# The last 128 rows of the down weights as fifteen short loads in place of one

## The chip, the cores and the metric

The program runs on one core of one Trainium2 chip. The metric is the device time of one execution in microseconds; of several executions the median counts. Data come from device memory into the core's on-chip memory of 128 partitions, moved by 16 DMA engines. A load is issued by the sequencer of an engine (here nearly always SP) and is then carried out by the DMA engines without it.

## The reference

The kernel computes one decode step of a transformer block for a batch of 4 and a width of 512: attention over a cache of 8192 keys and values in 32 heads, then a gated feed-forward part with a hidden width of 1792.

```python
q = (layernorm(x) @ wq).reshape(B, 1, 32, 128).transpose(0, 2, 1, 3)
p = softmax(einsum("bhqd,bhkd->bhqk", q, k_cache) * 128 ** -0.5)
h = x + einsum("bhqk,bhkd->bhqd", p, v_cache) @ wo
n = layernorm(h)
out = h + (sigmoid(n @ w_gate) * (n @ w_up)) @ w_down      # w_down: 1792 x 512, bf16
```

The two caches hold 537 MB of bf16 numbers, and all weights together 14 MB. Each byte is used once.

## The kernel before, in words

The large buffer `KV` has three slots of 64 KB a partition. The 128 pairs of batch and head are taken in 32 groups of four; each group loads 8 MB of keys (`load_k`) and 8 MB of values (`load_v`) into a slot, DVE transposes the keys in place, PE forms the scores, DVE and ACT the softmax, PE the product with the values. Nearly all of these loads are issued by SP, in program order, on one queue, and each load waits only until its slot is free.

After the last group `load_weights` issues the remaining weights on the same queue into the slots that are free by then: the output projection in two loads (`wo0`, `wo1`), gate (`wg`) and up (`wu`), and then the down weights in four loads `wd0` to `wd3` as `WD` sets it: 8, 4, 1 and 1 tiles of 128 rows. The first four wait for the last softmax (`t_a5`), the four of the down weights for the values product of the last group but one (`t_pv`). Rows of `w_down` are 1 KB. In `wd3` (tile 13, rows 1664 to 1791) row r goes to partition r of slot 2.

Each load has a semaphore of its own, which every load raises by 16 in all when it has landed: the 16 are the marks that the DMA engines taking part write behind their data, and what is missing to 16. `prog.dma` returns the value that a user of the data waits for; if several loads are given one name, the value counts them all.

At the end of the program PE runs the tail: the last group's values product (L399), the output projection (L457), layernorm, gate and up (L560), the turn of the hidden vector (L571) and the down product (L591). The down product takes the four pieces in order; its 56 products are four to a tile, and the first product of each piece waits for that piece's load (`t_w["wd0"]` to `t_w["wd3"]`). So the last four products wait for `wd3`. Behind them DVE (L601) and ACT (L602) copy the sums out of PSUM, and ACT issues the store of 4 rows of 1 KB (L603). SP's last instruction waits until it has landed (L605). Between the steps PE runs products of an identity (`fill`, L434) whose results nobody reads.

Of the kernel before, what the change touches and what calls it, by code (L numbers as in the profile page):

```python
# [88 lines left out]
def bass_sequential_preLN__mha_block_cached__glu_gated_glu__decode_kernel(  # L89
# [12 lines left out]
    B, _sq, D = A_x.shape  # L102
# [13 lines left out]
    prog = _Prog()  # L116
    emit = prog.emit

    with ExitStack() as es:
# [3 lines left out]
        def raw(t):  # L123
            return t.tensor if hasattr(t, "tensor") else t
# [31 lines left out]
        def kv(slot, off, inner, p0=0, np_=128):  # L156
            return bass.AP(raw(KV), p0 * KVROW + slot * SLOT + off, [[KVROW, np_], *inner])
# [145 lines left out]
        t_w = {}  # L303
# [2 lines left out]
        WG, WU = H * D, H * D + NDC * F  # L306
        assert WU + NDC * F <= SLOT

        def load_weights():
            w = [t_a5[NG - 1]]  # L310
            for i in range(2):
                t_w[f"wo{i}"] = prog.dma("sp", f"wo{i}", lambda e, i=i: e.dma_start(
                    kv(1, i * 16 * D, [[1, 16 * D]]),
                    A_wo[2048 * i:2048 * (i + 1), :].rearrange("(p k) f -> p (k f)", k=16)), w)
            for kind, mat, off, lo, hi in (("wg", B_w_gate, WG, 0, NDC), ("wu", B_w_up, WU, 0, NDC)):
                t_w[kind] = prog.dma("sp", kind, lambda e, mat=mat, off=off, lo=lo, hi=hi: e.dma_start(
                    kv(1, off + lo * F, [[1, (hi - lo) * F]]),
                    mat.rearrange("(p c) f -> p (c f)", p=128)[:, lo * F:hi * F]), w)
            w = [t_pv[NG - 2]]
            for i, (lo, hi) in enumerate(WD):  # L320
                if hi - lo > 1:
                    v = B_w_down[128 * lo:128 * hi, :].rearrange("(j x k) f -> x j (k f)", j=(hi - lo) // 4, k=4)
                    dst = kv(2, lo * D, [[4 * D, (hi - lo) // 4], [1, 4 * D]])
                else:
                    v, dst = B_w_down[128 * lo:128 * hi, :], kv(2, lo * D, [[1, D]])
                t_w[f"wd{i}"] = prog.dma("sp", f"wd{i}", lambda e, v=v, dst=dst: e.dma_start(dst, v), w)

        def transpose_k(g, i, keep):
            slot = kslot[g]
# [138 lines left out]
        for g in range(NG):  # L468
# [30 lines left out]
            if g == 0:  # L499
                load_k(2)  # L500
        load_weights()
        t_dm = emit("act", lambda e: e.activation(dummy[:, 0:1], TS[:, 4, 0:1], ACT.Sqrt), [t_et[NG - 1]])
        extract(NG - 2, True)
# [95 lines left out]
        def o_half(u):  # L599
# [3 lines left out]
        key, v = prog.dma("act", "out", lambda e: e.dma_start(  # L603
            out.rearrange("b s d -> (b s) d"), kv(0, 0, [[1, D]], 0, B)), [t_o])
# [33 lines left out]
```

## Time and profile before

| what | value |
|---|---|
| time, median of 3 runs | 1277.14 us (1277.12 to 1277.14) |
| span of the profiled execution, first to last instruction | 1275.6 us |
| share of the span in which the DMA engines were busy with SP's queue | 99.8% |
| bytes read, mean rate over the span | 550.77 MB, 432 GB/s |
| busy share of PE, DVE, ACT, POOL | 78%, 55%, 7%, 2% |
| mean granted TensorE clock | 0.918 |

The page gives the span of the profiled execution; its own time beyond the span is not shown. The median of the runs lies 1.5 us above the span, which is what stands around the first and the last instruction. In the profile an instruction is named by engine, line and operation; L326 is the line that issues the loads of the down weights and L591 the line of the down product. "DMA share" is the part of the 16 DMA engines that is busy in a stretch. A DMA's "time to landing" is counted from its issue to the last mark on its semaphore. Packets of 4 bytes are those marks, and are counted with the packets under 512 bytes.

### The profile page before, as it was taken

Reading aid. Unit: us, or ns where it says so; the run is one execution under the profiler, and the core shown is the slowest. Engines: PE = TensorE matmul, PEld = TensorE weight load, DVE = VectorE, ACT = ScalarE, POOL = GpSimd, SP = SyncE. Lnnn points to the kernel's source line nnn. Section 1 sums busy time; section 2 is a strip of 40 time slices with the busy share of each in tenths; the row PEclk is TensorE's granted clock in tenths of the full one; section 3 lists DMA queues with packets and bytes.
Section 4 is the critical chain, followed back from the end, with each engine's and each line's share of the span. In section 5 each row is a group of like instructions: output and inputs, shape, how many; then the busy total and the mean of one; then the engine's idle time right before and its main releaser. Section 6 shows DMA issues by size and latency. Waiting matters only on the chain. (4 is left out here: it accounts for less than half of the span.)

```text
span 1275.6 us, 10932 instructions
## 1 busy us (share of the span) xinstructions
PE 1001.2 (78%) x4450; PEld 409.7 (32%) x4450; DVE 701.8 (55%) x737; ACT 85.2 (7%) x202; POOL 22.6 (2%) x88
## 2 busy tenths in 40 slices
PE   1598777779777788777798777797777897777888
PEld 1233323333233333223333233333233332333334
DVE  0865665446655446654456654456554466544562
ACT  0000000000000000000000000000000000000010
POOL 1000000000000000000000000000000000000000
PEclk9899888899888898888998888998888998888989
DMA  9999999999999999999999999999999999999998
GB/s 420 434 425 434 427 444 432 430 438 427 442 434 430 438 427 444 432 432 436 427 444 432 432 436 434 438 432 434 434 434 438 432 436 432 436 436 430 440 430 371
DMA packets 10669, 550.95 MB, mean 432 GB/s; under 512 B 1176, under 2 KB 1440, under 8 KB 1824
## 3 DMA queue, kind: packets, MB, share of 16 engines
q1 hardware_dynamic: 10640, 550.77, 99.8%
q8 instruction: 8, 0.13, 0.0%
q14 instruction: 5, 0.04, 0.0%
q10 hardware_dynamic: 16, 0.01, 0.0%
HBM read 550.77 MB, written 0.00 MB: 432 GB/s over the span
## 5 line engine op out<-in xcount | busy, mean ns | idle before, releaser
L332 DVE STREAM_TRANSPOSE KV<-KV 128x2048 uint32<-128x2048 uint32 x256 | 568.6, 2279 | 379.1 <-DVEq L52 379.1
L342 PE MATMUL PS<-KV,Lq 128*128 128x512 bf16 x2048 | 543.6, 417 | 258.2 <-PEq L52 257.5
L385 PE MATMUL PS<-KV,PT 128*128 128x512 bf16 x1984 | 433.2, 379 | 0.0
L342 PEld LDWEIGHTS PS<-KV,Lq 128*128 128x128 bf16 x2048 | 199.8, 104 | 601.4 <-issue 442.7
L385 PEld LDWEIGHTS PS<-KV,PT 128*128 128x128 bf16 x1984 | 193.8, 98 | 234.5
L358 ACT ACTIVATE E_sb<-PS,TS 128x512 bf16<-128x512 f32 x32 | 22.0, 688 | 1124.6 <-DVE TS L357 1124.6
L352 DVE TENSOR_REDUCE TS<-PS 128x1 f32<-128x512 f32 x32 | 22.1, 692 | 70.4 <-DVEq L52 70.4
L369 ACT ACTIVATE PT<-ET 32x256 bf16<-32x256 bf16 x128 | 52.9, 413 | 30.8 <-DVE ET L361 28.5
L361 DVE STREAM_TRANSPOSE ET<-E_sb 128x512 bf16<-128x512 bf16 x32 | 22.8, 711 | 30.7 <-DVEq L52 30.7
L412 DVE STREAM_TRANSPOSE OX<-PS 128x512 f32<-128x512 f32 x31 | 20.9, 675 | 8.6 <-DVEq L52 8.6
L282 POOL TENSOR_TENSOR Lq<-q_all,mask 128x16 bf16<-128x16 bf16 x32 | 8.4, 263 | 575.0 <-DVE TS L357 563.4
L286 POOL COPY OT<-OTs 128x4 bf16<-128x4 bf16 x30 | 5.8, 192 | 622.3 <-DVE OTs L415 622.3
L434 PE MATMUL PS<-identf 128*128 128x512 f32 (+3 forms) x30 | 13.3, 551 | 0.0
L253 PE MATMUL PS<-xnT,KV 128*128 128x4 bf16 x128 | 3.6, 166 | 9.4 <-DMA KV<-in_A_wq_dram 9.4
L353 DVE STREAM_TRANSPOSE TS<-TS 128x32 f32<-128x32 f32 x32 | 6.8, 211 | 5.1 <-DVEq L52 0.6
L357 DVE STREAM_TRANSPOSE TS<-TS 128x32 f32<-128x32 f32 x32 | 6.8, 211 | 4.7
L374 DVE STREAM_TRANSPOSE TS<-TS 128x32 f32<-128x32 f32 x32 | 6.8, 211 | 4.7
L415 DVE TENSOR_SCALAR OTs<-Or,small 128x4 bf16<-128x4 f32 x30 | 6.9, 229 | 4.5 <-DVEq L52 1.4
L373 DVE COPY TS<-small 128x32 f32<-128x32 f32 x32 | 5.8, 182 | 6.2 <-DVEq L52 3.0
L355 DVE TENSOR_SCALAR TS<-small 128x32 f32<-128x32 f32 x32 | 5.8, 181 | 4.8 <-DVEq L52 0.2
L414 DVE TENSOR_REDUCE Or<-OX 128x4 f32<-128x16 f32 x31 | 5.6, 179 | 4.5
L354 DVE TENSOR_REDUCE small<-TS 128x1 f32<-128x16 f32 x32 | 5.4, 170 | 4.7
(87 smaller groups left out, 78.1 us busy)
## 6 DMA issues: line engine op xcount, KB each, us to landing
KV<-in_A_wq_dram SPq DMA_DIRECT2D x1, 4096.0 KB, 12.4
KV<-in_A_wo_dram SPq DMA_DIRECT2D x2, 2048.0 KB, 22.1
KV<-in_B_w_gate_dram SPq DMA_DIRECT2D x1, 1792.0 KB, 28.2
KV<-in_B_w_up_dram SPq DMA_DIRECT2D x1, 1792.0 KB, 32.0
KV<-in_B_w_down_dram SPq DMA_DIRECT2D x1, 1024.0 KB, 24.2
KV<-in_A_k_cache_dram SPq DMA_DIRECT2D x32, 32.4
KV<-in_A_v_cache_dram SPq DMA_DIRECT2D x32, 34.3
KV<-in_B_w_down_dram SPq DMA_DIRECT2D x1, 512.0 KB, 25.0
```

The lines of the kernel that those rows point to most:

```text
L282: emit("pool", lambda e: e.tensor_tensor(dst, src, msk, ALU.mult), [t_q, t_mk, t_lq0, t_a5.get(g - 1), t_oc.get(g - 3)], key="lq")
L332: emit("dve", lambda e: e.transpose(v, v), key="tp", take=take, keep=keep)
L342: ins = e.matmul(S_b[0], Lq[:, hp, 15 - s:15 - s + 128], rhs, start=(s == 0 and hp == 0), stop=(s == NS - 1 and hp == 3))
L352: dv(lambda e: e.tensor_reduce(TS[:, 0, 0:1], S_b[0], AX.X, ALU.max), [t_ts0] if g == 0 else [], [("sc", 1)])
L353: dv(lambda e: e.transpose(TS[:, 1, :], TS[:, 0, :]))
L358: emit("act", lambda e: e.activation(E_sb[:, :], S_b[0], ACT.Exp, bias=TS[:, 3, 0:1], scale=SCALE, accum_out=TS[:, 4, 0:1]), [t_a5[g]], ke ...
L361: t_et[g] = dv(lambda e: e.transpose(ET[:, :], E_sb[:, :]), take=[("ex", 1)], key="dve")
L369: emit("act", lambda e, dst=dst, src=src: e.activation(dst, src, ACT.Copy), [t_et[g], t_pt0 if g < NG - 1 else t_ptl], key="pt")
L385: ins = e.matmul(O_b, PT[:, u3, off:off + 128], rhs, start=(j == 0 and rl == 0), stop=(j == 3 and rl == NS - 1))
L412: emit("dve", lambda e: e.transpose(OX[:, :, :].rearrange("p (r i) x -> p r i x", r=4), src), w, key="dv", take=take, keep=keep)
L415: t_ox[g] = emit("dve", lambda e: e.tensor_scalar(dst, Or[:, :], small[:, 2 + g % 3:3 + g % 3], None, op0=ALU.mult), take=[("dv", 1)], kee ...
L434: ins = e.matmul(bk[:, 0:cols], identf[:, :], bass.AP(raw(identf), 0, [[128, 128], [0, cols // 128], [1, 128]]), start=True, stop=True, sk ...
```

## The change

The loads `wd0`, `wd1` and `wd2` stay as they are. The one load of `wd3` becomes fifteen loads, each of whole rows that follow one another: 15 rows, 14, 13 and so on down to 2, and one of 9, together 128. They go to the same places and are issued one after another by SP in place of the one. All raise the same semaphore, and the down product's last piece waits for the sum, 15 times 16.

```diff
+        def A_wd_rows(t, r, n):
+            return B_w_down[128 * t + r:128 * t + r + n, :]
+
...
-                t_w[f"wd{i}"] = prog.dma("sp", f"wd{i}", lambda e, v=v, dst=dst: e.dma_start(dst, v), w)
+                if i < 3:
+                    t_w[f"wd{i}"] = prog.dma("sp", f"wd{i}", lambda e, v=v, dst=dst: e.dma_start(dst, v), w)
+                    continue
+                r = 0
+                for n in [*range(15, 1, -1), 9]:
+                    t_w["wd3"] = prog.dma("sp", "wd3", lambda e, r=r, n=n: e.dma_start(
+                        kv(2, lo * D, [[1, D]], r, n), A_wd_rows(lo, r, n)), w)
+                    r += n
+                assert r == 128
```

On SP's queue the end of the program stands as follows before (a row is line, what is written and read, and partitions by elements; `x2` is two in a row):

```order
L299 DMA KV<-in_A_v_cache_dram 128x32768
L312 DMA KV<-in_A_wo_dram 128x8192 x2
L316 DMA KV<-in_B_w_gate_dram 128x7168
L316 DMA KV<-in_B_w_up_dram 128x7168
L326 DMA KV<-in_B_w_down_dram 128x2x2048
L326 DMA KV<-in_B_w_down_dram 128x2048
L326 DMA KV<-in_B_w_down_dram 128x512 x2
```

And this is the same place after, from `wd2` on, up to the load of 5 rows (those of 4, 3, 2 and 9 rows follow; `wd2` is L330 now and the short loads are L334):

```order
L330 DMA KV<-in_B_w_down_dram 128x512
L334 DMA KV<-in_B_w_down_dram 15x512
L334 DMA KV<-in_B_w_down_dram 14x512
L334 DMA KV<-in_B_w_down_dram 13x512
L334 DMA KV<-in_B_w_down_dram 12x512
L334 DMA KV<-in_B_w_down_dram 11x512
L334 DMA KV<-in_B_w_down_dram 10x512
L334 DMA KV<-in_B_w_down_dram 9x512
L334 DMA KV<-in_B_w_down_dram 8x512
L334 DMA KV<-in_B_w_down_dram 7x512
L334 DMA KV<-in_B_w_down_dram 6x512
L334 DMA KV<-in_B_w_down_dram 5x512
```

Nothing else moves on SP: the fifteen stand where the second load of 128 rows of 512 stood, and behind them comes only the wait for the store. On PE the tail of the down product (after the change it is L602) keeps its order and its waits, with the same rows as before but for the line:

```order
L602 MATMUL PS<-KV,ET 4x128 [waits s_wd0,s_dve]
L602 MATMUL PS<-KV,ET 4x128 x31
L602 MATMUL PS<-KV,ET 4x128 [waits s_wd1]
L602 MATMUL PS<-KV,ET 4x128 x15
L602 MATMUL PS<-KV,ET 4x128 [waits s_wd2]
L602 MATMUL PS<-KV,ET 4x128 x3
L602 MATMUL PS<-KV,ET 4x128 [waits s_wd3]
L602 MATMUL PS<-KV,ET 4x128 x3
```

No row moved here; the last wait is for another value of `s_wd3`, 240 where it was 16.

## The prediction

> **What bounds the kernel now.** I read the page first: the span, the row of DMA shares over 40 slices, and the queues.
>
> ```profile
> span 1275.6 us, 10932 instructions
> DMA  9999999999999999999999999999999999999998
> q1 hardware_dynamic: 10640, 550.77, 99.8%
> ```
>
> The DMA engines are busy from the first slice to the last, and 99.8% of that is SP's one queue. The stream of loads is the bound, and the changed load is its last. So the question is the end of the stream: when does it land, and is anyone waiting? Next I read SP's issues near the end, then the issue and landing of the last load alone (a window around its issue), then PE's weight loads of the down product in four short windows.
>
> ```profile
> 1237.14 0.43 SPq L316 DMA_DIRECT2D KV<-in_B_w_up_dram  x1
> 1247.43 1.84 SPq L326 DMA_DIRECT2D KV<-in_B_w_down_dram  x4
> ...
> L326 SPq DMA_DIRECT2D KV<-in_B_w_down_dram x1: 420/420/420, 1248.9 to 1248.9; - x1
> DMA to landing us min/median/max: 24.6/24.6/24.6
> ...
> 1273.26 0.36 PEld L591 LDWEIGHTS PS<-KV,ET 128*4 128x4 bf16 x8
> ...
> 1273.32 0.09 PEld L591 LDWEIGHTS PS<-KV,ET 128*4 128x4 bf16 x2
> ...
> 1273.53 0.09 PEld L591 LDWEIGHTS PS<-KV,ET 128*4 128x4 bf16 x4
> ```
>
> SP issues the four loads of the down weights in 1.84 us, 0.46 us each. The last is issued at 1248.9 and lands 24.6 us later, at 1273.5. PE's weight loads come in pairs: one pair at 1273.26, the next at 1273.32, so the next was due at about 1273.37. It starts at 1273.53. The last four products thus wait 0.16 us, and they start as `wd3` lands. The view of waits doesn't name this, since the gap is so short, but it settles the case: the end of the program hangs on the landing of `wd3`. A later landing moves the end by as much; an earlier one gains at most 0.16 us.
>
> How do the 16 DMA engines end? This table by stage has, at its end, the granted clock, the share of DMA engines that are busy, and GB/s:
>
> ```profile
> 1271.25:1271.50 0.25, 0.25 (x13) 0.25 (x12) 0.00 (x0) 0.00 (x0) 0.00 (x0) 1.00 0.98 377
> 1271.50:1271.75 0.25, 0.25 (x8) 0.25 (x5) 0.05 (x1) 0.00 (x0) 0.00 (x0) 1.00 0.89 348
> 1271.75:1272.00 0.25, 0.25 (x4) 0.08 (x5) 0.17 (x1) 0.00 (x0) 0.00 (x0) 1.00 0.63 250
> 1272.50:1272.75 0.25, 0.25 (x16) 0.25 (x12) 0.00 (x0) 0.00 (x0) 0.00 (x0) 1.00 0.60 209
> 1272.75:1273.00 0.25, 0.25 (x16) 0.22 (x12) 0.00 (x0) 0.00 (x0) 0.00 (x0) 1.00 0.34 119
> 1273.00:1273.25 0.25, 0.25 (x16) 0.25 (x12) 0.00 (x0) 0.00 (x0) 0.00 (x0) 1.00 0.30 86
> 1273.25:1273.50 0.25, 0.25 (x14) 0.15 (x6) 0.00 (x0) 0.00 (x0) 0.00 (x0) 1.00 0.00 0
> ```
>
> They don't end together. All are busy until 1271.5; then some six of 16 run dry within half a microsecond (share 0.98 to 0.63); about ten go on until 1272.75; the last ends before 1273.25, some 0.3 us ahead of the landing that PE sees. The first engine is done some 1.6 us before the last. `wd3` lands when the last one has, so what counts is which engines get more rows than now, the early or the late ones.
>
> **The change part by part.**
>
> *Fourteen more issues on SP.* At 0.46 us each, fifteen end at 1248.9 + 15 × 0.46 = 1255.8 us. The engines have older work until 1271.5 at the earliest (share 0.98), so the issues are hidden by 15 us of queued transfers, and nothing stands behind them on SP but the wait for the store. The cover fails only if one issue takes more than (1271.5 − 1248.9) / 15 = 1.5 us. Cost taken: none.
>
> *How rows are dealt out.* The trace holds two transfers of few rows: x, 4 rows of 1 KB, at the start, and the store, 4 rows of 1 KB, at the end. The store in slices of 5 ns (DMA share in tenths, then packets) and x in slices of 4 ns (GB/s):
>
> ```profile
> DMA  0005000000060000005100000060000000100000
> DMA packets 8, 0.00 MB, mean 21 GB/s; under 512 B 4, under 2 KB 8, under 8 KB 8
> q10 hardware_dynamic: 8, 0.00, 6.6%
> ...
> GB/s 0 0 0 0 0 0 256 0 256 0 0 0 0 8192 0 0 8193 8192 513 0 0 0 0 0 0 0 8192 0 2 0 8192 0 0 8192 0 0 0 0 0 0
> ```
>
> Four rows make four data packets and four marks: one engine a row. So I take it that a load of n rows below 16 uses n engines with one row and one mark each, where the load of 128 rows gave every engine 8 rows and one mark. [...]
>
> If the n engines are always the first n, the loads of 15 to 2 rows and of 9 give the sixteen engines 15, 15, 14, 13, 12, 11, 10, 9, 8, 6, 5, 4, 3, 2, 1 and 0 rows, 128 in all.
>
> *Price of a row.* From a stretch of the tail in which nearly all packets are such rows:
>
> ```profile
> DMA packets 99, 0.09 MB, mean 134 GB/s; under 512 B 14, under 2 KB 99, under 8 KB 99
> q1 hardware_dynamic: 99, 0.09, 38.8%
> ```
>
> It is 0.65 us long: 38.8% of 16 × 0.65 us is 4.04 us for 85 rows and 14 marks, 47 ns a row with marks thrown in. The store gives 6.6% of 16 × 0.2 us = 0.21 us for 4 rows with a mark each, 53 ns. Before: 8 × 47 = 0.38 us an engine. After: the fullest has 15 × 53 = 0.80 us, 0.42 us more; the emptiest saves 0.38 us.
>
> *The sum from below.* If the early engines are the fullest, they have 1.6 us to spare and use 0.42, the late ones lose rows, and the landing comes up to 0.38 us earlier, of which PE can use 0.16. Low end: −0.16 us.
>
> *The sum from above.* If the fullest are the last to end, the landing is 0.42 us later. There is one more thing: neighbouring rows may not go in parallel. The store's four rows start at slices 3, 11, 18 and 26, 38 ns apart, one after another though four engines move them; x starts two (slices 6 and 8) and then two more 40 ns later (513 in slice 18). [...] If four engines stood in line for each row, a row would take 4 × 38 = 152 ns, fifteen 2.28 us, and the landing would come up to 2.28 − 0.38 = 1.9 us later. High end: +1.9 us.
>
> [...]
>
> I take +0.35 us. It is nearest to the +0.42 of a full engine: engines reach the short loads spread over 1.6 us, so that lines of four will be rare, and an engine that falls behind its neighbour no longer meets it. It is a little below, since not every late engine can be a full one.
>
> *Behind the landing* nothing changes: products, copies and the store follow as they do now.
>
> The sum against the profiled execution: 1275.6 + 0.35 = 1275.95 us of span; on the median of the runs, which lies 1.5 us above it, 1277.14 + 0.35 = **1277.5 us**.
>
> **The rivals.** What a measurement of this kernel can tell from no change is about 0.2%, 2.55 us, so most of these end on the same side.
>
> *The early engines are the full ones.* Then the taper levels the tail: an engine that ends 1.6 us early takes 0.42 us more, and the late ones end up to 0.38 us earlier. For it: the stagger is large and in two bands, and the rows fall off evenly. Against: nothing shows that the early band is where the long loads begin. Time: 1277.14 − 0.16 = 1277.0 us.
>
> *Lines at the destination.* Most short loads go through one narrow place, as the store's rows do, and late engines are among them. For it stand the 38 ns steps. Against: x moved its rows in pairs, and the engines arrive spread. Taking half of the bound of 1.9: 1278.1 us. [...]
>
> *SP is held because too many loads are in the queue.* This is the one that ends on the slower side. At its longest the queue now holds nine loads: the last values, two of the output weights, gate, up and the four of down. It would hold 21 at 1255.8 us (fifteen, plus `wo1`, gate, up and three of down), and the trace never shows more than nine. These rows tell when older loads make room:
>
> ```profile
> KV<-in_B_w_gate_dram SPq DMA_DIRECT2D x1, 1792.0 KB, 28.2
> KV<-in_B_w_up_dram SPq DMA_DIRECT2D x1, 1792.0 KB, 32.0
> 1274.30 0.28 ACTq L603 DMA_DIRECT2D out_dram<-KV  x1
> ...
> L326 SPq DMA_DIRECT2D KV<-in_B_w_down_dram x2: 432/450/469, 1247.9 to 1248.4; - x2
> DMA to landing us min/median/max: 24.8/24.9/25.0
> ```
>
> Up lands at 1237.1 + 32.0 = 1269.1; the last two rows are `wd1` and `wd2`, which land between 1272.7 and 1273.3. If nine were the limit, only one short load could follow each landing: the first six or eight would be out by 1273.2, and the other seven would be issued from there at 0.46 us each, until 1276.4; a load on an idle queue needs about the store's 1.3 us (1274.30 to the span's end, 1275.6), so the landing would be at 1277.7, 4.2 us late: 1281.3 us. With room for sixteen the last would wait for `wd1`, to about 1272.9, and land at 1274.2, +0.7 us. It decides against "no change" only with a limit of eleven or less. Against it: the ninth load was issued as fast as the others (420 ns in the row of the last load), with no sign of being held.
>
> *An instruction fetch falls into the tail.* SP's program gets 14 loads longer. The profile has fetches of 16 KB on the same DMA engines:
>
> ```profile
> q8 instruction: 8, 0.13, 0.0%
> ...
> q8 instruction: 2, 0.03, 0.5%
> ```
>
> The second row is of 1240 to 1262 us: 0.5% of 16 × 22 us is 1.76 us for two, 0.9 us each. One more on a late engine would add up to 0.9 us: 1278.0 us. Eight fetches in the whole run make that unlikely.
>
> **How the numbers follow.** A landing later by 0 to 0.6 us, rows falling on early and late engines alike: 0.55, with 1277.1 to 1277.7. Full engines early: 0.21, 1277.0. Lines at the destination: 0.12, about 1278.1. A held SP: 0.08, of which 0.06 past 1279.7. A fetch: 0.04, about 1278.0. The range takes in the gain of 0.16 us, the forecast, the fetch and the lower part of the lines, 1276.95 to 1278.4, and leaves out the held SP and the upper part of the lines. Slower by over 0.2% is the held SP, 0.06; faster by over 0.2% would need 2.55 us where 0.16 us of waiting is all there is to win, 0.01; the rest is within 0.2%, 0.93.
>
> **What would show it.** In the profile after: fifteen issues on SP of about 0.46 us, ending near 1256 us; if one lasts longer or a gap opens among them, SP is held. The packets on q1 grow by 112: `wd3` has 128 marks, one a row, where it had 16. The DMA share after 1271.5: a single fall near 1273 means that the early engines took the rows; a long low tail past 1273.25 means that the late ones did, and its length is the loss. The last four weight loads of the down product, due at 1273.37 and now at 1273.53, show the price directly: at 1273.9 I am right, at 1273.4 the rival with the early engines is, beyond 1274.5 lines or a held queue. I would be wrong altogether if the loads before it changed their pace.

## The result, and the profile after

| | before | after |
|---|---|---|
| time, median of 20 runs each | 1277.14 us (1276.83 to 1277.37) | 1279.18 us (1278.95 to 1279.38) |
| span of the profiled execution | 1275.6 us | 1277.8 us |

The ratio is 1.0016, 95% interval 1.0009 to 1.0023: 2.04 us slower, 0.16%. No run of the one overlaps a run of the other. The forecast was 1277.5 us in a range up to 1278.4; the time lies 0.8 us above the range.

The page after, span and queue:

```profile
span 1277.8 us, 10946 instructions
q1 hardware_dynamic: 10752, 550.77, 99.6%
```

The queue carries the same bytes in 112 packets more, the 112 new marks. PE's weight loads in the down product (L602 now) and SP's issues near the end:

```profile
1271.99 0.87 PEld L602 LDWEIGHTS PS<-KV,ET 128*4 128x4 bf16 x32 [0.17 <-DVE ET L592]
1273.03 0.54 PEld L602 LDWEIGHTS PS<-KV,ET 128*4 128x4 bf16 x20 [0.17 <-DMA KV<-in_B_w_down_dram]
1275.73 0.09 PEld L602 LDWEIGHTS PS<-KV,ET 128*4 128x4 bf16 x4 [2.16 <-DMA KV<-in_B_w_down_dram]
...
1247.48 1.37 SPq L330 DMA_DIRECT2D KV<-in_B_w_down_dram  x3
1248.90 15.28 SPq L334 DMA_DIRECT2D KV<-in_B_w_down_dram  x15
```

The first 32 weight loads run when they did before (1271.99, where it was 1271.97), and the next 20 some 0.17 us later (1273.03, where it was 1272.87), since `wd1` landed that much later (1272.99, where it was 1272.83). The last four, at 1273.53 before, start at 1275.73: 2.20 us later, and the idle time ahead of them ends with a DMA. The span grew by those 2.2 us. So the loss is the wait for `wd3`. The table by stage for the same place (granted clock, share of busy DMA engines and GB/s at the end of each row):

```profile
1272.75:1273.00 0.25, 0.25 (x12) 0.12 (x6) 0.00 (x0) 0.00 (x0) 0.00 (x0) 1.00 0.47 140
1273.00:1273.25 0.25, 0.25 (x10) 0.22 (x10) 0.00 (x0) 0.00 (x0) 0.00 (x0) 1.00 0.46 127
1273.25:1273.50 0.25, 0.25 (x18) 0.25 (x12) 0.00 (x0) 0.00 (x0) 0.00 (x0) 1.00 0.04 12
1273.50:1274.00 0.50, 0.26 (x10) 0.07 (x4) 0.00 (x0) 0.00 (x0) 0.00 (x0) 1.00 0.00 0
1274.00:1275.00 1.00, 0.00 (x0) 0.00 (x0) 0.00 (x0) 0.00 (x0) 0.00 (x0) 1.00 0.00 0
```

Here is the riddle. By the packets of SP's queue the DMA engines are done at 1273.43, 0.2 us later than before (1273.19), where the forecast gave a full engine 0.42 us. Then no packet of the queue is recorded for over two microseconds, and PE still waits. SP issued the fifteen loads in 15.28 us, 1.0 us each and not 0.46, but it was done at 1264.2. The chain that ended last puts all of the time from there to the landing into one row, which is easily misread as a slow transfer:

```profile
1263.17 12.52 DMA KV<-in_B_w_down_dram
1275.69 0.04 issue
1275.73 0.30 PE PS L602 x4
```

Most of these 12.5 us are time in the queue behind older loads: the last of those, `wd2`, landed at 1273.35.

### The profile page after: what moved, and what is told of

It is laid out like the page before. It is cut to its first block, busy times and chain, and to the rows that moved or that the text cites. A ratio compares the mean times of both kernels' runs of the same rounds, so it can differ in the third digit from the quotient of the medians.

```text
span 1277.8 us, 10946 instructions
## 1 busy us (share of the span) xinstructions
PE 1001.5 (78%) x4450; PEld 409.9 (32%) x4450; DVE 701.7 (55%) x737; ACT 85.2 (7%) x202; POOL 22.6 (2%) x88
```

## The experiments

The theories that the runs were to tell apart: M, every DMA engine writes its marks one after another, some 0.18 us apart; S, all marks queue up at the one semaphore; P, neighbouring rows stand in line at their destination; R, the uneven number of rows is the cost. All edits are to the changed kernel unless another is named, and each run computes all that the kernel computes. Times are medians, with the kernel before in the same batches at 1277.05 to 1277.15 us. Some intervals reach 1; there the runs themselves decide: all runs of the kernel before lie at or below 1277.44 us, and all runs with four or more short loads at or above 1277.96.

**Eight loads of 16 rows: as many marks, dealt out evenly.**

```diff
-                for n in [*range(15, 1, -1), 9]:
+                for n in [16] * 8:
```

> Eight loads of 16 rows in place of the fifteen: 128 marks as after the change, but 8 on every DMA engine, and 8 rows on every engine as before. Theory M (each engine writes its marks one after another, about 0.18 us apart, a mark waiting until its rows are confirmed): the last engine's first mark at about 1273.2 us, seven more 0.18 us apart, landing about 1274.45, 0.95 us later than before: 1278.1 us. Rival S (128 marks queue up at the one semaphore): as after the change, +2.0, 1279.2 us. Rival P (several engines stand in line at neighbouring rows): sixteen neighbours at a time, as after the change or more, 1279.2 us or above. Rival R (the uneven rows alone): +0.1, 1277.2 us.

Measured: 1278.26 us, ratio 1.0009 (0.9999 to 1.0019), +1.18 us. Rows are even and the marks are 128, and the loss is a little over half. This is near M's 1278.1 and far from S, P and R. The last weight loads:

```profile
1274.98 0.09 PEld L602 LDWEIGHTS PS<-KV,ET 128*4 128x4 bf16 x4 [1.32 <-DMA KV<-in_B_w_down_dram]
```

**The same with every eighth row.**

```diff
-                r = 0
-                for n in [*range(15, 1, -1), 9]:
...
+                for j in range(8):
+                    t_w["wd3"] = prog.dma("sp", "wd3", lambda e, j=j: e.dma_start(
+                        bass.AP(raw(KV), j * KVROW + 2 * SLOT + lo * D, [[8 * KVROW, 16], [1, D]]),
+                        B_w_down[128 * lo:128 * hi, :].rearrange("(n s) f -> s n f", s=8)[j]), w)
```

> Eight loads of 16 rows again, but each takes every eighth row, so that the rows written side by side lie eight partitions apart. M: the same as with neighbouring rows, 1278.1 us. S: 1279.2 us. P: the line is gone, at most +0.2, 1277.3 us.

Measured: 1278.30 us, ratio 1.0009 (1.0000 to 1.0019). The place of the rows changes nothing, 0.04 us. P falls.

**A semaphore for each of the fifteen loads.**

```diff
-                r = 0
-                for n in [*range(15, 1, -1), 9]:
-                    t_w["wd3"] = prog.dma("sp", "wd3", lambda e, r=r, n=n: e.dma_start(
-                        kv(2, lo * D, [[1, D]], r, n), A_wd_rows(lo, r, n)), w)
+                r, t_w["wd3"] = 0, []
+                for j, n in enumerate([*range(15, 1, -1), 9]):
+                    t_w["wd3"].append(prog.dma("sp", f"wd3_{j}", lambda e, r=r, n=n: e.dma_start(
+                        kv(2, lo * D, [[1, D]], r, n), A_wd_rows(lo, r, n)), w))
...
-            t_d = emit("pe", f_down, [t_hh, t_w[f"wd{i}"]])
+            t_d = emit("pe", f_down, [t_hh, *(t_w["wd3"] if i == 3 else [t_w[f"wd{i}"]])])
```

> The fifteen loads as in the change, each with a semaphore of its own, all fifteen waited for. M: the chain of marks is on the DMA engine, so nothing changes: 1279.2 us. S: the queue at the semaphore is gone: at most +0.4, 1277.2 to 1277.5 us. P: 1279.2 us. The landing of each load shows the chain: under M the last ten or so land 0.18 us apart.

Measured: 1279.53 us, ratio 1.0019 (1.0009 to 1.0028), +2.45 us. With the marks spread over fifteen semaphores nothing is won, so S falls. The last mark comes at 1275.61 here and the weight loads start at 1275.86, 0.25 us behind it where the changed kernel has 0.04: PE now passes a wait for each of fifteen semaphores, which may be the reason. The run has a second use: each semaphore's record of marks is now that of one load. Of the last four loads, the times in us at which their marks came (SP's own share of the 16 left out):

```
load of 4 rows: 1273.802 1274.198 1274.889 1275.435
load of 3 rows: 1273.980 1274.369 1275.059
load of 2 rows: 1274.157 1275.229
load of 9 rows: 1273.289 1273.475 1274.351 1274.497 1274.550 1275.147 1275.324 1275.409 1275.612
```

A load of n rows has n marks (the nine rows have nine), and the same engines can be followed downwards. One marks at 1273.802, 1273.980 and 1274.157, 0.18 us from load to load; another at 1274.889, 1275.059 and 1275.229, 0.17 us. One is a microsecond ahead of the other, though both take part in every load. By the packets all of this data had been moved by 1273.5.

The engine that ends last, at 1275.612, marked 0.18 us earlier in the load of 4 rows, at 1275.435, and has no mark in those of 3 and 2. Followed back from there, it has a mark in each longer load, 0.17 to 0.20 us from one to the next. So it takes part in the loads of 15 to 4 rows and in that of 9: thirteen marks. The two engines with fifteen, which mark in every load, end at 1274.351 and 1275.409.

**Four loads of 32 rows, and two of 64.** Now fewer marks, with two and four rows ahead of each.

```diff
+                for n in [32] * 4:
```

> Four loads of 32 rows: 4 marks on each engine with two rows before each. M: three gaps of 0.18 us behind the first mark in place of the six rows that filled them, landing about +0.3, 1277.4 us. S (64 marks): about half of the loss, +1.0, 1278.1 us. R: 1277.1 us.

Measured: 1278.17 us, ratio 1.0008 (0.9998 to 1.0018), +1.02 us; M had said +0.3, S +1.0. By the time alone this run would speak for S. In the profile the last weight loads stand 0.64 us later than before, a span of 1276.2; the rest of the +1.02 lies outside the profiled span (the profiled execution took 1278.05 us, 1.85 us more than its span; all ten runs of this variant have 1.79 to 1.96 us there, and those of the other variants 1.26 to 1.60). That part I can't place.

```profile
1274.17 0.09 PEld L602 LDWEIGHTS PS<-KV,ET 128*4 128x4 bf16 x4 [0.61 <-DMA KV<-in_B_w_down_dram]
```

```diff
+                for n in [64] * 2:
```

> Two loads of 64 rows: 2 marks on each engine with four rows, about 0.17 us, before each. M: one gap of 0.18 us that four rows fill anyway: +0.0 to +0.1, 1277.1 to 1277.2 us. S (32 marks): +0.5, 1277.6 us.

Measured: 1277.48 us, ratio 1.0003 (0.9994 to 1.0013): no change that can be told from none, though the +0.33 us is more than M gave. By the trace `wd2` landed 0.2 us later here than before, and `wd3` 0.36 us behind it, where it was 0.34.

**Sixteen loads of 8 rows: all marks on eight engines.**

```diff
+                for n in [8] * 16:
```

> Sixteen loads of 8 rows: 128 marks, 16 on each of eight DMA engines, none on the others. M: if a late engine is among the eight, its first mark at about 1273.1 and fifteen more 0.18 us apart, landing about 1275.85, +2.4, 1279.5 us; if all eight are early ones, first mark about 1272.0, landing about 1274.7, +1.2, 1278.3 us. S: as after the change, 1279.2 us. R: 1277.1 to 1277.5 us.

Measured: 1279.80 us, ratio 1.0021 (1.0012 to 1.0031), +2.65 us; M with a late engine among the eight had 1279.5.

```profile
1276.48 0.09 PEld L602 LDWEIGHTS PS<-KV,ET 128*4 128x4 bf16 x4 [2.88 <-DMA KV<-in_B_w_down_dram]
```

**Uneven rows with few marks.**

```diff
+                for n in [88, 40]:
```

> [...] M: four rows more on a late engine, 0.17 us, and a mark: +0.1 to +0.35, 1277.2 to 1277.5 us. R (the uneven rows are the loss): 4 of the 7 rows that the fullest engine gained, about +1.2, 1278.3 us. [...]

Measured: 1277.38 us, ratio 1.0002 (0.9993 to 1.0012), +0.23 us. The two loads have 88 and 40 rows, and the queue has 5 packets more than before, 21 marks for 16. That fits 11 engines with 8 rows and then 10 with 4. Which engines those are no run shows; that ten of them have 12 rows instead of 8, as the expectation's sums take it, is an estimate. By it the uneven rows cost what four packets cost (0.19 us at 47 ns), or nothing. R, which gave 1278.3, falls.

**Thirty-two loads of 4 rows: the same 128 marks on four engines.** M was put into a number now: n marks on the fullest engine take n × 0.183 us.

```diff
+                for n in [4] * 32:
```

> Thirty-two loads of 4 rows: again 128 marks in all, but 32 on each of four DMA engines and none on the other twelve. M, with the numbers of the runs so far (each mark 0.183 us behind the one before): 32 x 0.183 = 5.86 us in place of the 0.34 us of eight rows and a mark, so +5.5 us behind a late engine and +4.0 behind an early one: 1281 to 1283 us. S (a queue at the semaphore, set by the 128 marks): as after the change, 1279.2 us. SP needs 32 issues of about 1 us, until about 1282 us if it is held as long at each; under M with a held SP the end could come a few us later still, and the issues in the profile tell.

Measured: 1282.65 us, ratio 1.0044 (1.0027 to 1.0061), +5.60 us. SP's 32 issues took 22.4 us and were out by 1271.3, so SP isn't what the end waits for. The last weight loads, SP's issues, and the packets between 1275.0 and 1276.6:

```profile
1279.14 0.09 PEld L602 LDWEIGHTS PS<-KV,ET 128*4 128x4 bf16 x4 [5.66 <-DMA KV<-in_B_w_down_dram]
...
1248.86 22.39 SPq L334 DMA_DIRECT2D KV<-in_B_w_down_dram  x32
...
DMA packets 36, 0.02 MB, mean 11 GB/s; under 512 B 19, under 2 KB 36, under 8 KB 36
q1 hardware_dynamic: 36, 0.02, 12.9%
```

Here the rows themselves have become slow: 12.9% of 16 × 1.6 us is 3.3 us for 17 rows and their marks, 0.19 us a row where it was 0.047. In the trace's packets 62 of the 128 short rows, some fifteen for each of the four engines, still take 0.05 us, and the other 66 take 0.17 to 0.19. So in this run an engine gets some fifteen loads ahead of its marks, and from there on its rows go at the pace of the marks. The last row is moved by 1276.7, and the last mark comes 2.4 us behind it.

The semaphore's record ends in one engine's marks, 0.18 us apart:

```
1278.188 1278.369 1278.552 1278.734 1278.917 1279.099
```

The starts of the last four weight loads, run by run, make a line:

| marks on the fullest engine | loads | start, us | step for one mark |
|---|---|---|---|
| 4 | 4 of 32 rows | 1274.17 | |
| 8 | 8 of 16 | 1274.98 | 0.81 / 4 = 0.20 us |
| 16 | 16 of 8 | 1276.48 | 1.50 / 8 = 0.19 us |
| 32 | 32 of 4 | 1279.14 | 2.66 / 16 = 0.17 us |

From 8 to 32 marks it is 4.16 / 24 = 0.17 us a mark, with 128 marks, 128 rows and one semaphore in all three. The changed kernel, with 15 on the fullest engine, stands at 1275.73, below the line at 15 (about 1276.3), since its last engine to end isn't one of the two with fifteen but, if it is the one that ends last with fifteen semaphores, has thirteen.

The start of the weight loads also holds what the loads ahead were late. Counted from the landing of `wd2` to the last mark of `wd3`, by the semaphores' records, it is 0.34 us before, 0.75 with 4 marks, 1.50 with 8, 3.09 with 16 and 5.84 with 32: 0.18 to 0.19 us for each mark in all four. In the changed kernel it is 2.34 us, 0.18 us for each of thirteen. The four loads of 32 rows then make 0.75 − 0.34 = 0.41 us, and `wd2` landed 0.22 us later there than before: that is the 0.64 of their profile, and S isn't needed for it.

**The fifteen loads ahead of the others.** Is the chain of marks a mere delay beside which other rows move, or does it hold up the engine?

```diff
-            for i, (lo, hi) in enumerate(WD):
+            for i, (lo, hi) in [(3, WD[3]), *enumerate(WD[:3])]:
...
-                    t_w["wd3"] = prog.dma("sp", "wd3", lambda e, r=r, n=n: e.dma_start(
+                    t_w["wd3"] = prog.dma("sp", "wd3", lambda e, r=r, n=n, lo=lo: e.dma_start(
```

> The fifteen loads are issued ahead of the other three down loads and not behind them. M: the marks are a chain of latencies beside the data that follow; by the time the last load has moved they are written, and its own mark is one: 1277.0 to 1277.4 us. If the chain holds up the engine's data as well, every later load is late by as much, and the end is as after the change, 1279.2 us. P, a loss of rate in the engines: 1278.5 to 1279.2 us. S: 1277.2 us, as M.

Measured: 1278.71 us, ratio 1.0014 (1.0004 to 1.0023), +1.63 us. Not hidden: M's first sentence is wrong here, and its second is nearer. (P's 1278.5 to 1279.2 has the time too, but P has fallen with the rows eight partitions apart.) The products of the first piece now wait for `wd0`, and rows are still being moved long past 1273.5. Weight loads and products, then the table by stage:

```profile
1273.58 0.90 PEld L602 LDWEIGHTS PS<-KV,ET 128*4 128x4 bf16 x32 [1.38 <-issue]
1273.61 1.99 PE L602 MATMUL PS<-KV,ET 128*4 128x128 bf16 x56 [1.22 <-DMA KV<-in_B_w_down_dram]
1274.76 0.65 PEld L602 LDWEIGHTS PS<-KV,ET 128*4 128x4 bf16 x24 [0.28 <-DMA KV<-in_B_w_down_dram]
...
1273.00:1273.50 0.50, 0.00 (x0) 0.00 (x0) 0.00 (x0) 0.00 (x0) 0.00 (x0) 1.00 0.41 156
1273.50:1274.00 0.50, 0.39 (x14) 0.42 (x16) 0.00 (x0) 0.00 (x0) 0.00 (x0) 1.00 0.22 84
1274.00:1274.75 0.75, 0.67 (x25) 0.48 (x18) 0.00 (x0) 0.00 (x0) 0.00 (x0) 1.00 0.10 37
```

**The control: the one whole load ahead of the others**, made from the kernel before with the same change of order.

> The kernel before with its last load issued ahead of the other three down loads, whole, as one load: the control for the run with the fifteen loads in front. If the marks were the cost there (engines held up by their chain, rows behind them late), the order alone costs nothing: 1277.0 to 1277.3 us. If the order was the cost, as in that run: 1278.7 us.

Measured: 1277.25 us, ratio 1.0001 (0.9992 to 1.0011). The order costs nothing that can be told from none. By the packets the last rows are moved by 1273.1 us here and by 1274.7 with the fifteen ahead. So the +1.63 us are the short loads, and an engine with a chain of marks also moves the rows behind it late. In the changed kernel the chain has fifteen loads at most and no row stands behind it, so the packets look done at 1273.43 and only the marks are late, until 1275.69.

## Why the prediction was wrong

*What bounds the end* was right and carried the rest: the end hangs on the landing of `wd3`, a later landing moves it by as much. PE's last weight loads moved by 2.20 us and the span by 2.2.

*The price of a row* is the step that failed. "The fullest has 15 × 53 = 0.80 us" took the busy time of packets, 46 ns for a row and 9 ns for a mark, as the time that an engine needs for them. As packets they did take about that, and the engines' packets ended 0.2 us later than before. But a load has landed when its marks are written (PE starts 0.04 us behind the last, which comes at 1275.69), and on one engine these come 0.17 to 0.20 us apart when there is only a row or two between them. Eight rows with one mark cover that with their own time (0.38 us in the prediction, 0.34 by the marks of `wd2` and `wd3`), so the trace of before couldn't show it; nor could the store or x, in which each engine wrote one mark. In place of the term +0.42 us belongs 13 × 0.18 − 0.34 = +2.0 us, for a last engine with thirteen marks, as the run with fifteen semaphores has it; another 0.2 us is that `wd2` landed later, at 1273.35 where it was 1273.15. Together that is the +2.2 of the profile.

The trace of before had a hint that I passed over: the queue's last packet ends at 1273.19, and the landing, at 1273.49, is 0.3 us behind it. That delay was known, and I took it for something paid once at the end. It isn't the 0.18 us from mark to mark, and no run shows how the two hang together; but it did say that a mark isn't there when its packet is done. The sign that I had set for a start beyond 1274.5, lines or a held queue, was wrong as well: the runs show neither as the cause.

As a packet a mark took 9 ns, yet from mark to mark on one engine there are 0.18 us. What the engine waits for in that time no run shows; that it is the confirmation of the rows, as theory M was put for the eight loads of 16 rows, was a supposition. The runs show the spacing, and that rows behind such a chain are late (the last at 1274.7 us with the fifteen loads ahead, at 1273.1 with the one whole load ahead). Nor does any run change the number of marks on an engine without that of the loads it takes part in. The moving of the short loads' rows isn't what costs in the changed kernel: by the packets its last rows follow one another 0.048 us apart and are done by 1273.42.

*The range.* Its upper bound of +1.9 us came from lines at the destination, four engines in line for each row. The measured 2.04 us is near that number, but the mechanism isn't it: rows eight partitions apart cost the same to 0.04 us. In the chances, lines got 0.12 and half of their bound; the true cause wasn't among the rivals.

*How rows are dealt out* was right in number: n rows have n marks, as the run with fifteen semaphores shows. It also shows early and late engines among those that take part in every load, so that a falling number of rows could not level the end of the engines; that rival is out. That the n engines are always the first n was a supposition, and the runs identify engines by their marks only, not by number; two engines with fifteen marks and one with thirteen agree with the counts worked out from it.

*SP held.* The rival came about in part: the fifteen issues took 15.28 us, though not by the limit on the number of loads that it supposed (see the end). By itself it cost nothing, as the part on the fourteen issues said: the last was out at 1264.2, 7 us before the queue ran dry. The run with 8 × 16 rows was out at 1257.8 and lost 1.18 us all the same, and the loads of 88 and 40 rows, of 6.64 us, lost next to nothing.

*An instruction fetch in the tail* plays no part that the runs show: there are eight fetches of 16 KB on q8 in both profiles, and the loss follows the number of marks.

*The sign at 0.2%* came out as said, within 0.2%, at 0.16%; the time didn't.

## What to carry to other kernels

Count the marks on the fullest DMA engine of what the end waits for, not the packets' busy time: a mark cost some 0.18 us there unless its own rows took longer (eight rows and a mark took 0.34 us). That is measured here on loads into on-chip memory issued by SP, with rows of 1 KB. A last load should be cut only while each engine still has several rows for each mark; two loads of 64 rows of 1 KB were the limit here: they cost 0.33 us, which can't be told from none, and four of 32 rows 1.02 us, 0.64 of them in the profile. And when a queue looks idle while its reader waits, look at when the semaphore was raised before looking for a lost transfer.

## What I had not expected

A chain of marks isn't only a delay at the end: put ahead of other loads, the fifteen held up the rows behind them and cost 1.63 us, against 0.2 us, which can't be told from none, for the same 128 rows in one load. And with 32 on an engine, the short loads' own rows went at the pace of the marks.

SP's issues became slow, and not for being short: behind the other loads a short issue took 1.02 us in the middle of fifteen, but ahead of them fifteen took 5.67 us, 0.25 to 0.40 each, and the three loads behind them then took 6.60 us. These are SP's issues in the run with the fifteen ahead:

```profile
1247.44 5.67 SPq L334 DMA_DIRECT2D KV<-in_B_w_down_dram  x15
1253.15 6.60 SPq L330 DMA_DIRECT2D KV<-in_B_w_down_dram  x3
```

So the length of an issue isn't a matter of the load's size alone, and what sets it no run shows. The number of loads on the queue doesn't explain it: in the changed kernel SP was held at the second short load (2.20 us), the tenth on its queue, and with the fifteen ahead it issued them all behind the five older loads, and `wd0` behind them in 0.41 us, before `wd1` and `wd2` took 1.61 and 4.50. In the changed kernel it cost nothing, with 7 us of older work left behind the last issue.

Two things stay open: the part of the loss with four loads of 32 rows that lies outside the profiled span, and some 0.2 us by which `wd1` and `wd2` landed later in the profiles of most variants than in that of before.
